# Clustered attention and two feed-forward layers on one core: values and sums in four 32-column strips, one sum for both halves

## The chip, the cores and the metric

The kernel runs on one core of a Trainium2 chip. The metric is the device time of one launch in microseconds (us), here the median of three runs. The engines are TensorE (PE in the profile, PEld for its weight loads), VectorE (DVE), ScalarE (ACT), GpSimd (POOL) and SyncE (SP, which issues the transfers). All of them run their own instruction streams and wait for one another through semaphores.

## The reference

Attention with clusters, then two feed-forward layers, all in float32. Batch 2, 8 heads, 768 positions, 64 values per head, 16 clusters.

```python
q_assign = argmax(einsum('bhsd,hcd->bhsc', q_n, c_n))      # the same for k
mask = q_assign[:, :, :, None] == k_assign[:, :, None, :]
scores = where(mask, scale * (q @ k.T), -1e9)
attn = exp(scores - max(scores))
attn = attn / (attn.sum(-1) + 1e-9)
x = (attn @ v)                                              # to (1536, 512)
h = x @ w_in                                                # 512 -> 2048
g = where(h >= 1, h, where(h <= -1, 0, (h + 1) ** 2 / 4))
x = g @ w_out                                               # 2048 -> 512
xn = x / rms(x) * rms_g
out = (silu(xn @ w_gate) * (xn @ w_val)) @ w_out2           # 512 -> 1536 -> 512
```

## The kernel before

The 16 pairs of batch and head are worked on two at a time: a pair `p` (0 to 7) holds two heads `h`. Its 768 queries are cut into two halves of 384 (`HALF`), its 768 keys into six tiles of 128 (`kt`). A step `i` of a pair is one half and one key tile, so a pair has 12 steps; steps are counted through all pairs as `g` (0 to 95).

In one step `score` (L376) makes, for each head, a 128x384 tile of scores by two matmuls (L382, L383, the second adds the rows of the maxima), and ScalarE takes the exponential into a tile `P` of its own per head (L385, 14 buffers). GpSimd adds the six `P` of a half and head into `acc` (L391, L395). `values` (L397) multiplies `P` by v: each head writes 64 rows of the PSUM tile `pv`, with 64 weight columns (L403); both heads' matmuls run side by side in the array. A float32 matmul is two instructions, two passes over the columns. `values_out` (L414) copies `pv` to SBUF as `pvs`. When a half is through, `sums` (L419) adds `acc` over the 128 partitions by a matmul with a 128x64 tile of ones: each head fills 64 rows of the PSUM tile `sum`, the sum repeated in each row. `finish` (L425) makes the reciprocal and the quotient in six pieces: 0 is logarithm and exponential on ScalarE (L434, L435), 1 and 2 correct it on VectorE in PSUM (L437, L439), 3 multiplies it by the values (L442), 4 and 5 split the product into a rounded part on ScalarE (`xh`, L444) and the rest on VectorE (`xl`, L446), which are what the feed-forward projections read. The last pair takes its sums directly from `P` (L411).

Around this, each step also searches the maxima of a later pair (`maxq` L313: two matmuls L333 into two PSUM banks, each emptied by a VectorE reduction, L335; a bank is written again for the next step only after its reduction), and `prep` (L145) prepares a still later pair: similarities in four strips of 32 columns (L168), a one-hot code on VectorE (L192 to L209), a split of q and k with a subtraction on GpSimd (L160), and copies by transfers on SP's queue (L67).

The order is written out by hand. `attention_steps` (L897) takes two or three steps at a time; three (`by_three`) from step 24 to 83. Of such a group the order on TensorE is: maxima and scores of the first step, scores with the maxima between them of the second, scores and then maxima of the third, and then `values_of` (L886), which puts the sums that are due ahead of the values of the group before. After each step `other_engines` (L862) issues the pieces of `finish` that are due: they are listed as distances `d` from the last step `s` of the half. Piece 0 comes right after the sums in groups of three, and piece 4 at the head of a group. Since each engine's queue is in order, a piece on VectorE stands ahead of the reductions of the step that follows. From step 84 on weights of the feed-forward layers are converted between the steps, and from step 92 some projections (L583) stand between the groups. After step 101 only feed-forward work is left.

Of the kernel before, what the change touches and what calls it, by code (L numbers as in the profile page):

```python
# [9 lines left out]
F32 = mybir.dt.float32  # L10
# [11 lines left out]
DM = H * D  # L22
# [15 lines left out]
def clustered_attention_two_ffn(  # L38
# [43 lines left out]
    ones = cp.tile([128, 64], F32, name="ones")  # L82
# [32 lines left out]
    def p_tile(name, dt=F32):  # L115
        return ap.tile([128, HALF], dt, tag="P", bufs=14, name=name)

# [19 lines left out]
    def one_rows():  # L137

        row = BB[0][96:97, 0, 1]
        nc.scalar.copy(row.rearrange("p (a b) -> p a b", b=64), ones[96:97].unsqueeze(1).to_broadcast([1, S // 64, 64]))  # L140
        copy(BB[0][96:97, 1, 1], row)
        for t in BB[1:]:
            copy(t[96:97, :, 1], row.unsqueeze(1).to_broadcast([1, 2, S]))
# [232 lines left out]
    def score(p, i, h):  # L376
# [7 lines left out]
        P = p_tile(f"P{p}_{i}_{h}")  # L384
        nc.scalar.activation(P, sc, AF.Exp, scale=0.125)  # L385
        st["P", p, i, h] = P
        if p == NP - 1:
            return
        if kt == 1:
            acc = ap.tile([128, HALF], F32, tag="acc", bufs=4, name=f"acc{p}_{i}_{h}")  # L390
            nc.gpsimd.tensor_tensor(acc, st["P", p, i - 1, h], P, op=ALU.add)  # L391
            st["acc", p, half, h] = acc
        elif kt > 1:
            acc = st["acc", p, half, h]
            nc.gpsimd.tensor_tensor(acc, acc, P, op=ALU.add)  # L395

    def values(p, i):  # L397
# [4 lines left out]
        for h in range(2):  # L402
            nc.tensor.matmul(pv[64 * h:64 * h + 64, 0:HALF], st["v", p][:, h, kt], st["P", p, i, h],  # L403
                             start=(kt == 0), stop=(kt == NT - 1))

        if p == NP - 1:
# [3 lines left out]
            for h in range(2):  # L410
                nc.tensor.matmul(st["sm", p, half][64 * h:64 * h + 64], ones, st["P", p, i, h],  # L411
                                 start=(kt == 0), stop=(kt == NT - 1))

    def values_out(p, half):  # L414
        x = ap.tile([128, HALF], F32, tag="fin", bufs=4, name=f"pvs{p}_{half}")
# [3 lines left out]
    def sums(p, half):  # L419
        sm = misc(f"sum{p}_{half}", "sum")[:, 0:HALF]  # L420
        for h in range(2):
            nc.tensor.matmul(sm[64 * h:64 * h + 64], ones, st["acc", p, half, h], start=True, stop=True)  # L422
        st["sm", p, half] = sm

    def finish(p, half, piece):  # L425
        b, hp = divmod(p, 4)
        sm = st["sm", p, half]
        cs = slice(S * b + HALF * half, S * b + HALF * half + HALF)
        xh, xl = XH[:, hp, cs], XL[:, hp, cs]

# [716 lines left out]
```

## Time and profile before

| | |
|---|---|
| median of three runs | 791.8 us (791.02 to 791.87) |
| span of the profiled execution | 789.3 us |
| TensorE busy | 783.0 us (99%) |
| VectorE busy | 569.1 us (72%) |
| ScalarE busy | 353.4 us (45%) |
| GpSimd busy | 167.6 us (21%) |
| mean granted TensorE clock | 1.000 |

The page gives the span from the first to the last instruction; the time of the profiled execution around it isn't given. Busy time is the union of an engine's instructions. The ends of matmuls are modelled, so the distance from start to start tells more of TensorE than busy time does. The attention stage fills the first 235 us or so, the rest is feed-forward work.

### The profile page before, as it was taken

The page shows a single profiled execution, that of the slowest core. Times are in us where ns is not written, and L with a number is a line of the kernel's source. Part 1 is how long each engine was busy: PE and PEld are TensorE (multiplying, and loading weights), DVE is VectorE, ACT ScalarE, POOL GpSimd, SP SyncE. Part 2 cuts the span into 40 slices and gives each one's busy share as a digit, 9 for nine tenths or more (in the row PEclk, how much of TensorE's full clock was granted, in tenths as well). Part 3 has the DMA queues.
Part 4 walks back from the last instruction along what each step waited for, and adds up shares of the span by engine and source line. Part 5 has one row for each costly group of instructions (what it writes and reads, how often), then busy time and mean ns, then how long its engine had stood idle before and what let it go on. Part 6 is the DMA issues. An engine that isn't in the chain of part 4 may idle for free.

```text
span 789.3 us, 10670 instructions
## 1 busy us (share of the span) xinstructions
PE 783.0 (99%) x3786; PEld 605.9 (77%) x3786; DVE 569.1 (72%) x1081; ACT 353.4 (45%) x666; POOL 167.6 (21%) x186
## 2 busy tenths in 40 slices
PE   8999999999999999999999999999999999999998
PEld 4666676676568888888888878888888888888887
DVE  6767787776676878777778788988777888733333
ACT  7676676765566555434444435333333222211110
POOL 5878999997000000000000000000000000000000
PEclk9999999999999999999999999999999999999999
DMA  7756675581333555454443520536555544200003
GB/s 201 175 138 171 161 179 123 138 215 38 107 120 106 173 175 165 158 158 150 143 137 130 161 81 27 159 108 196 175 190 187 159 153 149 73 1 1 1 32 129
DMA packets 32677, 103.40 MB, mean 131 GB/s; under 512 B 5016, under 2 KB 5356, under 8 KB 32624
## 3 DMA queue, kind: packets, MB, share of 16 engines
q1 hardware_dynamic: 32612, 102.72, 44.0%
q8 instruction: 30, 0.49, 0.3%
q14 instruction: 23, 0.19, 0.1%
q10 hardware_dynamic: 12, 0.00, 0.0%
HBM read 81.02 MB, written 3.15 MB: 107 GB/s over the span
## 4 chain that ended last, share of the span: by engine, by line
PE 92%; DVE 4%; ACT 3%; issue 0%; ACTq 0%; DVEq 0%
PE h L583 38%; PE y L631 9%; PE y L632 9%; PE y L633 9%; PE pv L403 8%; PE mp L333 5%; PE sc L382 4%; PE sc L383 4%; PE sum L422 1%; DVE a L603 1%; PE simt L168 1%; ACT a L599 1%; ACT a L598 1%; PE xt L701 1%; PE sum L411 1%; PE oht_ps L219 0%
## 5 line engine op out<-in xcount | busy, mean ns | idle before, releaser
L335 DVE TENSOR_REDUCE M<-mp 128x1 f32<-128x384 f32 x186 | 94.5, 551 | 43.8 <-PE mp L333 43.6
L583 PE MATMUL h<-xh,aa 128*128 128x512 f32 x360 | 116.0, 391 | 0.1
L395 POOL TENSOR_TENSOR acc<-acc,P 128x384 f32<-128x384 f32 x112 | 109.3, 1010 | 4.1 <-ACT P L385 3.5
L583 PE MATMUL h<-xh,bb 128*128 128x512 f32 x312 | 100.9, 389 | 0.1
L385 ACT ACTIVATE P<-sc 128x384 f32<-128x384 f32 x192 | 82.4, 490 | 40.1 <-PE sc L383 32.8
L583 PE MATMUL h<-xh,place 128*128 128x512 f32 x288 | 92.7, 389 | 0.0
L534 ACT ACTIVATE raw<-raw 128x512 f32<-128x512 f32 x62 | 42.1, 679 | 107.7 <-DVE bits L532 105.4
L648 DVE TENSOR_TENSOR Y<-y,Y 128x512 f32<-128x512 f32 (+1 forms) x85 | 57.7, 680 | 31.2 <-PE y L633 31.2
L583 PEld LDWEIGHTS h<-xh,aa 128*128 128x128 f32 x360 | 67.6, 188 | 16.0 <-issue 1.2
L403 PE MATMUL pv<-P,v 128*64 128x384 f32 x384 | 70.6, 492 | 0.0
L583 PE MATMUL h<-xl,aa 128*128 128x512 f32 x180 | 70.1, 389 | 0.0
L583 PEld LDWEIGHTS h<-xh,bb 128*128 128x128 f32 x312 | 58.5, 188 | 12.7 <-DVE bb L546 0.6
L382 PE MATMUL sc<-aa,bb 112*128 112x384 f32 x192 | 66.2, 345 | 0.0
L383 PE MATMUL sc<-aa,bb 97*128 97x384 f32 x192 | 65.0, 338 | 0.0
L603 DVE SCALAR_TENSOR_TENSOR a<-h,a 128x512 f32<-128x512 f32 x48 | 33.1, 690 | 41.9 <-ACT a L599 41.7
L583 PEld LDWEIGHTS h<-xh,place 128*128 128x128 f32 x288 | 54.0, 188 | 11.3
L583 PE MATMUL h<-xl,bb 128*128 128x512 f32 x156 | 60.7, 389 | 0.0
L583 PE MATMUL h<-xl,place 128*128 128x512 f32 x144 | 56.0, 389 | 0.0
L333 PE MATMUL mp<-bb,aa 112*128 112x384 f32 x186 | 52.5, 360 | 0.3
L403 PEld LDWEIGHTS pv<-P,v 128*64 128x64 f32 x384 | 25.4, 136 | 31.5 <-issue 30.3
L532 DVE SCALAR_TENSOR_TENSOR bits<-raw,bits 128x512 uint32<-128x512 uint32 x68 | 46.8, 688 | 1.3
L608 ACT CAST bb<-a 128x512 fp32r<-128x512 f32 x34 | 21.1, 622 | 53.2 <-DVE a L606 33.5
(207 smaller groups left out, 1538.4 us busy)
## 6 DMA issues: line engine op xcount, KB each, us to landing
raw<-w_out SPq DMA_DIRECT2D x28, 512.0 KB
mid<-w_out SPq DMA_DIRECT2D x28, 511.8 KB
raw<-w_in SPq DMA_DIRECT2D x16, 512.0 KB
mid<-w_in SPq DMA_DIRECT2D x16, 511.8 KB
raw<-w_gate SPq DMA_DIRECT2D x12, 512.0 KB
raw<-w_val SPq DMA_DIRECT2D x12, 512.0 KB
mid<-w_gate SPq DMA_DIRECT2D x12, 511.8 KB
mid<-w_val SPq DMA_DIRECT2D x12, 511.8 KB
```

Source lines behind the costliest of these rows:

```text
L333: nc.tensor.matmul(mp, A[0:112, h, 0, 128 * qt:128 * qt + 128], Bk[0:112, h, 0, HALF * n:HALF * n + HALF], start=True, stop=True)
L335: nc.vector.tensor_reduce(st["M2", p][:, j, n:n + 1], mp, axis=AX.X, op=ALU.max)
L382: nc.tensor.matmul(sc, Bk[0:112, h, 0, ks], A[0:112, h, 0, qs], start=True, stop=False)
L383: nc.tensor.matmul(sc, Bk[0:97, h, 1, ks], A[0:97, h, 1, qs], start=False, stop=True)
L385: nc.scalar.activation(P, sc, AF.Exp, scale=0.125)
L395: nc.gpsimd.tensor_tensor(acc, acc, P, op=ALU.add)
L403: nc.tensor.matmul(pv[64 * h:64 * h + 64, 0:HALF], st["v", p][:, h, kt], st["P", p, i, h], start=(kt == 0), stop=(kt == NT - 1))
L583: nc.tensor.matmul(h, w[:, wi, fs], x[:, kc, cs], start=(n == 0), stop=(n == 11))
L631: nc.tensor.matmul(y[:, c], g[:, 0, fs], w[:, 0, c], start=(m == m0), stop=False)
L632: nc.tensor.matmul(y[:, c], g[:, 0, fs], w[:, 1, c], start=False, stop=False)
L633: nc.tensor.matmul(y[:, c], g[:, 1, fs], w[:, 0, c], start=False, stop=(m == ms[-1]))
L648: nc.vector.tensor_tensor(Y[:, c], y[:, c], Y[:, c], op=ALU.add)
```

## The change

Values and sums use four strips of 32 weight columns instead of two of 64. Strips 0 and 2 hold the first and second 32 values of head 0, strips 1 and 3 those of head 1, so that the rows of `pv` run head 0, head 1, head 0, head 1; the rows of `w_in` are put in the same order on the host. The sums of both halves of a pair are made at once: half 0 in rows 0 to 63 (32 for each head), half 1 in rows 64 to 127. Pieces 0 and 1 then run once for a pair. Piece 2 writes the reciprocals twice to SBUF (tiles `R`, one for each half), and a new piece 6 copies the 64 rows that a half has to the 64 that it lacks by a transfer within SBUF on SP's queue. Pieces 3 to 5 work on `pvs` in SBUF instead of on `sum` in PSUM. The two heads' `P` and `acc` share tiles, and GpSimd adds both in one instruction of 768 columns (apart in the first half of pair 0). The last pair keeps its way, in four strips. The distances of the pieces are set anew.

```diff
-    def p_tile(name, dt=F32):
-        return ap.tile([128, HALF], dt, tag="P", bufs=14, name=name)
+    def p_tile(name):
+        return ap.tile([128, 2, HALF], F32, tag="P", bufs=8, name=name)
...
+        apart = p == 0 and half == 0
+        hs = slice(h, h + 1) if apart else slice(0, 2)
+        if h == 0 and kt == 1:
+            st["acc", p, half] = ap.tile([128, 2, HALF], F32, tag="acc", bufs=3, name=f"acc{p}_{half}")
+        if h == 1 or apart:
+            acc = st["acc", p, half]
+            nc.gpsimd.tensor_tensor(acc[:, hs], (st["P", p, i - 1] if kt == 1 else acc)[:, hs], P[:, hs], op=ALU.add)
 
     def values(p, i):
...
-        for h in range(2):
-            nc.tensor.matmul(pv[64 * h:64 * h + 64, 0:HALF], st["v", p][:, h, kt], st["P", p, i, h],
-                             start=(kt == 0), stop=(kt == NT - 1))
+        strips = [(32 * c, c % 2, slice(32 * (c // 2), 32 * (c // 2) + 32)) for c in range(4)]
+        for r, h, d in strips:
+            nc.tensor.matmul(pv[r:r + 32, 0:HALF], st["v", p][:, h, kt, d], st["P", p, i][:, h],
+                             start=(kt == 0), stop=(kt == NT - 1), tile_position=(0, r))
...
-    def sums(p, half):
-        sm = misc(f"sum{p}_{half}", "sum")[:, 0:HALF]
-        for h in range(2):
-            nc.tensor.matmul(sm[64 * h:64 * h + 64], ones, st["acc", p, half, h], start=True, stop=True)
-        st["sm", p, half] = sm
+    def sums(p):
+        sm = misc(f"sum{p}", "sum")[:, 0:HALF]
+        for half in range(2):
+            for h in range(2):
+                r = slice(64 * half + 32 * h, 64 * half + 32 * h + 32)
+                nc.tensor.matmul(sm[r], ones, st["acc", p, half][:, h], start=True, stop=True,
+                                 tile_position=(0, r.start))
+        st["sm", p, 0] = sm
...
         elif piece == 2:
-            nc.vector.scalar_tensor_tensor(sm, sm, 2.0, st["r0", p], op0=ALU.subtract, op1=ALU.mult)
+            for i in range(1 if last else 2):
+                r = sm if last else ap.tile([128, HALF], F32, tag="R", bufs=2, name=f"R{p}_{i}")
+                nc.vector.scalar_tensor_tensor(r, sm, 2.0, st["r0", p], op0=ALU.subtract, op1=ALU.mult)
+                st["R", p, i] = r
         elif piece == 3:
-            nc.vector.tensor_tensor(sm, sm, st["pvs", p, half], op=ALU.mult)
+            if last:
+                nc.vector.tensor_tensor(sm, sm, st["pvs", p, half], op=ALU.mult)
+            else:
+                nc.vector.tensor_tensor(x, x, st["R", p, half], op=ALU.mult)
         elif piece == 4:
-            nc.scalar.activation(xh, sm, AF.Copy, scale=-1.0)
+            nc.scalar.activation(xh, x, AF.Copy, scale=-1.0)
+        elif piece == 6:
+            for i in range(2):
+                t = st["R", p, i]
+                nc.sync.dma_start(t[64 - 64 * i:128 - 64 * i], t[64 * i:64 * i + 64])
         else:
-            nc.vector.scalar_tensor_tensor(xl, sm, -1.0, xh.bitcast(F32), op0=ALU.mult, op1=ALU.subtract)
+            nc.vector.scalar_tensor_tensor(xl, x, -1.0, xh.bitcast(F32), op0=ALU.mult, op1=ALU.subtract)
...
-            for p in range(NP):
-                for half in range(2):
-                    s = 12 * p + 6 * half + 5
-                    ds = (3, 4, 4, 5, 5, 6) if p == NP - 1 else (None, 8, 9, 9, None, 10) if by_three(s) else (7, 8, 9, 10, None, 11)
-                    if ds[piece] == g - s:
-                        finish(p, half, piece)
+            for half in range(2):
+                s = 12 * NP - 7 + 6 * half
+                if (3, 4, 4, 5, 5, 6)[piece] == g - s:
+                    finish(NP - 1, half, piece)
+        for p in range(NP - 1):
+            s = 12 * p + 11
+            late = 3 * (p < NP - 2)
+            for d, half, piece in ((7, 0, 0), (8, 0, 1), (9, 0, 2), (10, 0, 6), (12 + late // 3, 0, 3), (13 + late // 3, 1, 3),
+                                   (14 + late, 0, 5), (16 + late, 1, 5)):
+                if d == g - s and (piece or not by_three(s)):
+                    finish(p, half, piece)
...
-            if 0 <= sp < NP - 1 and si in (5, 11):
-                sums(sp, si // 6)
+            if 0 <= sp < NP - 1 and si == 11:
+                sums(sp)
...
+        for k in range(g, g + n):
+            for half in range(2):
+                for fp_ in range(NP - 1):
+                    if k - 12 * fp_ - 11 == 13 + 3 * half + 3 * (fp_ < NP - 2):
+                        finish(fp_, half, 4)
...
+    def strips(w):
+        return w.reshape(H // 2, 2, 2, D // 2, -1).transpose(0, 2, 1, 3, 4).reshape(DM, -1)
...
-        "w_in": cols(a["moe_w_in"]),
+        "w_in": cols(strips(a["moe_w_in"])),
...
-    nc = _bacc.Bacc("TRN2", target_bir_lowering=False, num_devices=1)
+    nc = _bacc.Bacc("TRN2", target_bir_lowering=False, num_devices=1, dynamic_dma_scratch_size=1024)
```

Left out are the tile of ones (32 columns instead of 64), the same strips in the last pair's sums, the tags of `pvs` and `r0`, and the head of `finish`, which takes `x` as `pvs` of the half and, for the last pair, as `sum`.

## Rows read from the trace of the kernel before

**Rows 1.** The page: the span, and each engine's busy us, share, instructions.

```profile
span 789.3 us, 10670 instructions
PE 783.0 (99%) x3786; PEld 605.9 (77%) x3786; DVE 569.1 (72%) x1081; ACT 353.4 (45%) x666; POOL 167.6 (21%) x186
```

**Rows 2.** Busy time by stretch of the span; columns are in the first line.

```profile
core 0: us, PE busy (x) PEld busy (x) DVE busy (x) ACT busy (x) POOL busy (x), PEclk, DMA share, GB/s
85.00:202.00 117.00, 117.00 (x689) 79.75 (x688) 86.79 (x182) 76.70 (x176) 101.41 (x99) 1.00 0.56 138
```

**Rows 3.** Timeline of TensorE: start, duration (us), engine, line, operation, tiles, shape, count.

```profile
100.25 2.16 PE L403 MATMUL pv<-P,v 128*64 128x384 f32 x12
...
106.04 0.87 PE L422 MATMUL sum<-acc,ones 128*64 128x384 f32 x4
106.74 2.10 PE L403 MATMUL pv<-P,v 128*64 128x384 f32 x12
```

**Rows 4.** Timeline of TensorE, similarities of a later pair in four strips.

```profile
120.70 0.52 PE L168 MATMUL simt<-qraw,CB 128*32 128x384 f32 x2
120.71 0.52 PE L168 MATMUL simt<-kraw,CB 128*32 128x384 f32 x2
121.05 0.49 PE L168 MATMUL simt<-qraw,CB 128*32 128x384 f32 x2
...
121.48 0.44 PE L333 MATMUL mp<-bb,aa 112*128 112x384 f32 x1
```

**Rows 5.** Timeline, TensorE's weight loads for the values of two steps.

```profile
60.94 0.20 PEld L403 LDWEIGHTS pv<-P,v 128*64 128x64 f32 x4 [0.25 <-issue]
...
61.31 0.14 PEld L403 LDWEIGHTS pv<-P,v 128*64 128x64 f32 x2 [0.18 <-issue]
...
61.63 0.14 PEld L403 LDWEIGHTS pv<-P,v 128*64 128x64 f32 x2 [0.18 <-issue]
```

**Rows 6.** Timeline of GpSimd; in brackets idle time before, and what ended it.

```profile
91.33 6.80 POOL L395 TENSOR_TENSOR acc<-acc,P 128x384 f32<-128x384 f32 x7
99.28 1.02 POOL L391 TENSOR_TENSOR acc<-P,P 128x384 f32<-128x384 f32 x1 [1.15 <-ACT P L385]
...
104.95 5.85 POOL L395 TENSOR_TENSOR acc<-acc,P 128x384 f32<-128x384 f32 x6
```

**Rows 7.** Timeline, the first transfer and the instruction that it released.

```profile
0.74 0.39 SPq L108 DMA_DIRECT2D cw<-cent  x1
...
2.43 0.26 ACT L471 ACTIVATE cw<-cw 128x64 f32<-128x64 f32 x1 [0.42 <-DMA cw<-cent]
```

**Rows 8.** Timeline of VectorE in steps 39 to 44.

```profile
105.97 1.02 DVE L335 TENSOR_REDUCE M<-mp 128x1 f32<-128x384 f32 x2 [0.39 <-PE mp L333]
...
109.25 1.02 DVE L335 TENSOR_REDUCE M<-mp 128x1 f32<-128x384 f32 x2
110.19 0.55 DVE L209 TENSOR_TENSOR oh<-sim,m 128x384 bf16<-128x384 f32 x1
110.67 1.02 DVE L335 TENSOR_REDUCE M<-mp 128x1 f32<-128x384 f32 x2
```

**Rows 9.** Timeline of TensorE, maxima matmuls of steps 43 and 44.

```profile
110.29 0.51 PE L333 MATMUL mp<-bb,aa 112*128 112x384 f32 x2
...
111.70 0.52 PE L333 MATMUL mp<-bb,aa 112*128 112x384 f32 x2
```

**Rows 10.** Timeline of GpSimd and VectorE in the first 10 us.

```profile
5.20 0.82 POOL L965 CAST aa<-qhl 64x768 fp32r<-64x768 f32 x1 [2.04 <-ACT qhl L156]
6.08 1.45 POOL L261 CAST aa<-qhl 64x768 fp32r<-64x768 f32 x1
7.61 1.80 POOL L160 TENSOR_TENSOR khl<-kraw,khl 128x768 fp32r<-128x768 f32 x1
...
5.83 1.00 DVE L160 TENSOR_TENSOR qhl<-qraw,qhl 128x768 fp32r<-128x768 f32 x1
```

**Rows 11.** By line, two VectorE products of pair 0: ns least/median/most, first and last start.

```profile
L201 DVE TENSOR_TENSOR e<-eq,rank x1: 627/627/627, 9.0 to 9.0; 128x384 bf16<-128x384 bf16 x1
...
L209 DVE TENSOR_TENSOR oh<-e,m x1: 557/557/557, 10.3 to 10.3; 128x384 bf16<-128x384 bf16 x1
```

More of the change, by code (lines that the diff above doesn't have):

```diff
@@ L81, in clustered_attention_two_ffn @@
     ident_b = cp.tile([128, 128], BF16, name="ident_b")
-    ones = cp.tile([128, 64], F32, name="ones")
+    ones = cp.tile([128, 32], F32, name="ones")
     nc.vector.memset(ones, 1.0)
@@ L139, in one_rows @@
         row = BB[0][96:97, 0, 1]
-        nc.scalar.copy(row.rearrange("p (a b) -> p a b", b=64), ones[96:97].unsqueeze(1).to_broadcast([1, S // 64, 64]))
+        nc.scalar.copy(row.rearrange("p (a b) -> p a b", b=32), ones[96:97].unsqueeze(1).to_broadcast([1, S // 32, 32]))
         copy(BB[0][96:97, 1, 1], row)
@@ L383, in score @@
         nc.tensor.matmul(sc, Bk[0:97, h, 1, ks], A[0:97, h, 1, qs], start=False, stop=True)
[L384 to L387, printed above, removed]
-            return
[L389 to L395, printed above, removed]
+        if h == 0:
+            st["P", p, i] = p_tile(f"P{p}_{i}")
+        P = st["P", p, i]
+        nc.scalar.activation(P[:, h], sc, AF.Exp, scale=0.125)
+        if p == NP - 1 or kt == 0:
+            return
+        apart = p == 0 and half == 0
[5 more added lines that the diff above has]
+            nc.gpsimd.tensor_tensor(acc[:, hs], (st["P", p, i - 1] if kt == 1 else acc)[:, hs], P[:, hs], op=ALU.add)
     def values(p, i):
@@ L409, in values @@
                 st["sm", p, half] = misc(f"sum{p}_{half}", ("misc", "mx1")[half])[:, 0:HALF]
-            for h in range(2):
-                nc.tensor.matmul(st["sm", p, half][64 * h:64 * h + 64], ones, st["P", p, i, h],
-                                 start=(kt == 0), stop=(kt == NT - 1))
+            for r, h, d in strips:
+                nc.tensor.matmul(st["sm", p, half][r:r + 32], ones, st["P", p, i][:, h],
+                                 start=(kt == 0), stop=(kt == NT - 1), tile_position=(0, r))
     def values_out(p, half):
-        x = ap.tile([128, HALF], F32, tag="fin", bufs=4, name=f"pvs{p}_{half}")
+        x = ap.tile([128, HALF], F32, tag="pvs", bufs=4, name=f"pvs{p}_{half}")
         nc.scalar.copy(x, st["pv", p][:, 0:HALF])
         st["pvs", p, half] = x
-    def sums(p, half):
-        sm = misc(f"sum{p}_{half}", "sum")[:, 0:HALF]
-        for h in range(2):
-            nc.tensor.matmul(sm[64 * h:64 * h + 64], ones, st["acc", p, half, h], start=True, stop=True)
-        st["sm", p, half] = sm
+    def sums(p):
[6 more added lines that the diff above has]
+        st["sm", p, 0] = sm
     def finish(p, half, piece):
         b, hp = divmod(p, 4)
-        sm = st["sm", p, half]
+        last = p == NP - 1
+        sm = st["sm", p, half if last else 0]
         cs = slice(S * b + HALF * half, S * b + HALF * half + HALF)
         xh, xl = XH[:, hp, cs], XL[:, hp, cs]
+        x = sm if last else st["pvs", p, half]
         if piece == 0:
-            r0 = st["r0", p] = ap.tile([128, HALF], F32, tag="fin", bufs=4, name=f"r0{p}_{half}")
+            r0 = st["r0", p] = ap.tile([128, HALF], F32, tag="r0", name=f"r0{p}_{half}")
             nc.scalar.activation(r0, sm, AF.Ln, bias=eps9)
@@ L901, in attention_steps @@
             max_rows(*row, 1)
-        fp_, fi = divmod(g - (10 if n == 3 else 11), 12)
-        if 0 <= fp_ < NP - 1 and fi in (5, 11):
-            finish(fp_, fi // 6, 4)
+        for k in range(g, g + n):
[3 more added lines that the diff above has]
+                        finish(fp_, half, 4)
         for k in range(g, g + n):
```

2 lines of the change are left out of this document (1 added, 1 removed).

## The prediction, made before the changed kernel had been run

> **What bounds the kernel now.** I read the page first: TensorE is busy 783.0 of 789.3 us, VectorE 569.1, GpSimd 167.6 [rows 1]. GpSimd's small share hides a stage: by stretches, between 85 and 202 us TensorE has no idle time, while GpSimd works 101.41 of 117 us, VectorE 86.79 and ScalarE 76.70, with the granted clock at 1.00, the 2.4 GHz level [rows 2]. So in the attention stage TensorE sets the pace, GpSimd runs close behind, and VectorE has about 30 us of air, unevenly spread. The change touches only this stage; the projections behind it start earlier by whatever it saves. Where TensorE starts late on a VectorE result, that shows as an idle gap before a maxima matmul; in the stretch that I read instruction by instruction (97 to 122 us, one pair's period of 12 steps) there is none. Hence TensorE work taken out should count in full, and any new delay of VectorE beyond its cover counts in full too.
>
> **Part 1, sums (the gain).** A group of steps with a sum: its matmuls begin at 106.04 and the values at 106.74, and those last 2.10; without a sum the values last 2.16 [rows 3]. So a sum costs 0.70 - 0.06 = 0.64 us. Today each half of the seven pairs before the last has its sum, 14 in all; the change keeps seven. That takes out 7 x 0.64 = **4.5 us**, all on TensorE's path.
>
> **Part 2, four strips.** Half the columns per matmul, twice the matmuls. If strips run side by side, a pass over 384 columns costs the same. The similarity matmuls show four strips of 32: the first pass starts at 120.70, the second at 121.05, and all of one pass start together [rows 4]. For today's two strips of 64 the weight loads show the rhythm: 0.37 us from the first pass to the second, then 0.32 [rows 5]. I read 0.05 of the 0.37 as the first weight load, which nothing covers; for 32 columns it is then 0.35 - 0.32 = 0.03. Per entry that saves 0.03, and the last of four strips starts about 0.01 later than the last of two; 38 groups x 0.017 = 0.6 us gained. The similarity matmuls that follow values would no longer change strip width; leaving a width costs some 0.1 beyond a pass (121.48 less 121.05 is 0.43 [rows 4]), six times at most, so 0 to 0.6; I take 0.5. Together **-1.1 us**. The other end: a steady third pass of four strips is not in the trace. If every pass took 0.35 instead of 0.32, 216 passes (192 for values, 24 for the last pair's sums) would lose 0.025 x 216 = 5.4 us. I take the first end, since the longer interval is explained by its weight load.
>
> **Part 3, GpSimd's adds.** Two adds of 384 become one of 768 (five pairs at the start stay apart). Six adds in a row last 5.85, about 0.97 each [rows 6]; a subtraction of 768 lasts 1.80 [rows 10]. One for two saves about 0.1 us, some 6 us in all on GpSimd, which is not the bound. The sum now waits for an add that starts only with the second head and ends up to 1.80 - 0.97 = 0.8 later. Cover: the last add of a half ends at 91.33 + 6.80 = 98.13 [rows 6], its sum starts at 106.04 [rows 3], 7.9 us. Cost nothing; the larger ring of P tiles only loosens ScalarE.
>
> **Part 4, finishing.** ScalarE loses seven logarithm and exponential pairs, VectorE seven first corrections: idle time, no gain. The 14 transfers sit in SP's queue behind the second corrections, and place copies and weight loads wait behind them. A transfer is issued three steps (about 6 us) ahead of its reader, two for pair 6. The nearest landing: a first transfer issued at 0.74 releases ScalarE at 2.43, 1.7 us later [rows 7]. Hidden; were that cover gone, the product would stand on VectorE with the next reductions behind it, and TensorE behind those: up to about 1.7 us a pair. In the tail pair 6 finishes at step 97, while the projections of token block 0, which does not read it, are still on TensorE: nothing.
>
> What is not hidden is where VectorE's pieces land. Steps run in threes. Steps 39 to 41 have one piece in place of another, and the idle 0.39 before 105.97 takes it [rows 8]. But step 42 (as 30, 54 and 66) now has the low part and the one-hot ahead of the second pair of maxima: the reductions at 110.67 move by one piece (0.48 by 110.19 to 110.67), end at 112.17, and the second matmul of the pair at 111.70 is due at 111.87 [rows 8, 9]. That is 0.3 late in each of the four periods that have a one-hot, **+1.2 us**.
>
> **Part 5, VectorE against GpSimd.** The product (values times reciprocal) and the low part used to have one input in PSUM; now both are in SBUF. The trace has such instructions only in its first 10 us, and there they touch. GpSimd's copy of 64x768 takes 0.82 alone and 1.45 when VectorE's two-input subtraction (5.83 to 6.83) starts first [rows 10]: GpSimd stood until VectorE was done. The other way round, a two-input product of VectorE, begun while GpSimd's 1.8 us subtraction ran, took 627 ns against 557 for its neighbour [rows 10, 11]: 0.07 us lost.
>
> Nine such pieces lie where VectorE has little cover while GpSimd is busy: in four periods one before the one-hot chain (cover 0.2: the reductions at 109.25 end at 110.27, due 110.46 [rows 8, 9]) and one at step 42 (no cover left); in the fifth period one. The two earlier pieces of a period fall into GpSimd's pause (98.13 to 99.28 [rows 6]) or start just ahead of its next add. By the 0.07 of the nearest row: 9 x 0.07 = **+0.6 us**. The upper end is a wait for a whole add of 768, 1.8 by the subtraction's row: 9 x 1.8 less the cover of 0.2 at five of them, 15.2 us. I take the low end because it is the only row in that direction, and keep the other for the range.
>
> The Trainium skill, page "SBUF — State Buffer", section "Who interferes with whom", says that a VectorE instruction with two SBUF inputs contends with a GpSimd instruction that reads SBUF, and that whichever issues first blocks the other completely. By that rule VectorE would wait for the rest of an add, and the case called "port" below would hold; the 1.45 agrees with the rule in one direction, the 627 shows little of it in the other.
>
> **Sum.** -4.5 - 1.1 + 1.2 + 0.6 = -3.8 us. The profiled execution has a span of 789.3; its time around the span is not shown, so I carry over the 2.5 us between the span and the median of 791.8. Span after 785.5, time **788.0 us**.
>
> **Rivals.** *Port, bad phase (slower).* VectorE stands behind a whole add. GpSimd's adds follow each other without a pause, so the place in its cycle at which a piece arrives repeats from pair to pair. A piece at step 40 that just misses an add waits about 1.5, less 0.2 of cover, and one at step 42, half an add later, about 0.9: 4 x 2.2 + 0.7 = 9.5 instead of 0.6, so -3.8 + 8.9 = +5.1: 796.9. For it: the 1.45, GpSimd's 87% in this stretch, adds twice as long. Against: the 627. It decides from 0.5 us lost per piece (4.4 of net gain without the port, over nine).
> *Port, mean phase (no change).* Pieces arrive at random in a 1.8 us cycle of which the port is held for about 1.5 (an estimate: the product that began 0.4 before the subtraction's end lost only 0.07, so the end of it is free): mean wait 1.5 x 1.5 / (2 x 1.8) = 0.63, behind the cover 0.47; 4 x 1.1 + 0.5 = 4.9: 792.3.
> *Strips slower.* The 5.4 of part 2 instead of its 0.6: -3.8 + 6.0 = +2.2: 794.0, slower. Against it: strips of one pass start together today.
> That the change doesn't do what it says would need sums to wait for GpSimd; the 7.9 us speak against it, under 2 in 100.
>
> **How the numbers follow.** About 0.2% (1.6 us) is what a measurement here can tell from no change. Forecast 0.42, its own range 785.5 to 789.8; port in mean phase 0.20; port in bad phase 0.30; strips 0.08. Faster 0.42, same 0.20, slower 0.38. The range of 8 in 10 reaches from 785.4 (parts 1 and 2 with no late piece, 786.2, less 0.8, the spread of the three runs) to 797.7 (port in bad phase and the same 0.8).
>
> **What would show it.** Right: sums in seven groups instead of 14; passes of values 0.32 apart; no idle before maxima matmuls; products and low parts near 0.55 us. Port: those two lines at 1 us and more or with VectorE idle before them, and TensorE's maxima released by VectorE late at steps 30, 42, 54 and 66. Strips: passes 0.35 apart. I would be wrong altogether if a transfer came later than its reader, or if TensorE's gain vanished in a wait that no row here shows.

## Result and the profile after

The changed kernel takes 802.8 us (median; 799.3 to 803.0) against 791.8 us before: ratio 1.0127, 95% interval 1.0107 to 1.0147. It is slower by 11 us, where 788.0 was forecast and the range ended at 797.7. The profiled execution is the shortest of them, 799.34 us with a span of 797.5, 8.2 over before's span [rows 1]; the traces are compared on these two.

The page: span, then each engine's busy time. Below them, from TensorE's list of waits (us in total, times, longest), the two kinds that the kernel before does not have.

```profile
span 797.5 us, 11359 instructions
PE 784.4 (98%) x4218; PEld 602.0 (75%) x4218; DVE 574.9 (72%) x1074; ACT 347.5 (44%) x652; POOL 164.0 (21%) x121
...
PE mp L333 <- DVE M L335: 5.1, 5, 1.2
PE mp L333 <- DMA bb<-oht: 1.0, 2, 0.8
```

TensorE's maxima matmuls now wait for VectorE's maxima and for one-hot copies. Busy time by stretch answers [rows 2]: of the 117 us that TensorE filled before, 6.5 are idle.

```profile
core 0: us, PE busy (x) PEld busy (x) DVE busy (x) ACT busy (x) POOL busy (x), PEclk, DMA share, GB/s
85.00:202.00 117.00, 110.50 (x854) 72.87 (x855) 87.52 (x166) 67.44 (x155) 98.70 (x53) 0.99 0.59 146
...
85.00:88.10 3.10, 1.85 (x8) 1.28 (x8) 3.10 (x5) 1.80 (x5) 3.10 (x2) 1.00 0.97 203
88.20:91.60 3.40, 3.40 (x18) 1.26 (x22) 2.81 (x7) 0.00 (x0) 3.32 (x3) 0.50 0.86 225
```

The last row is a second loss. Behind a stretch in which TensorE was busy 1.85 of 3.10 us, its granted clock was 0.50, the 1.2 GHz level, from 88.2 to 91.6. At half speed 3.4 us of work is 1.7 us lost, by estimate. Three later waits of nearly the same length (1.22, 1.23 and 1.13 us, at 115.09, 140.63 and 167.94) were followed by no fall.

By line (busy us, mean ns of one): low part and product, after and then before; the sums, after and then before.

```profile
L463 DVE SCALAR_TENSOR_TENSOR xl<-pvs,xh 128x384 fp32r<-128x384 f32 x13 | 15.5, 1194 | 1.4 <-ACT xh L457 1.4
L455 DVE TENSOR_TENSOR pvs<-pvs,R 128x384 f32<-128x384 f32 x14 | 10.4, 740 | 0.0
...
L446 DVE SCALAR_TENSOR_TENSOR xl<-sum,xh 128x384 fp32r<-128x384 f32 x15 | 8.2, 548 | 3.5 <-ACT xh L444 3.5
L442 DVE TENSOR_TENSOR sum<-sum,pvs 128x384 f32<-128x384 f32 x16 | 9.0, 563 | 0.4
...
L426 PE MATMUL sum<-acc,ones 128*32 128x384 f32 x56 | 6.0, 498 | 0.0
L422 PE MATMUL sum<-acc,ones 128*64 128x384 f32 x56 | 12.1, 512 | 0.0
```

The sums came down as meant. The low part went from 548 to 1194 ns. One of its instructions, by the timelines of VectorE, GpSimd and TensorE (start, duration):

```profile
85.24 1.89 DVE L463 SCALAR_TENSOR_TENSOR xl<-pvs,xh 128x384 fp32r<-128x384 f32 x1
87.06 0.54 DVE L209 TENSOR_TENSOR oh<-sim,m 128x384 bf16<-128x384 f32 x1
87.53 1.00 DVE L335 TENSOR_REDUCE M<-mp 128x1 f32<-128x384 f32 x2
...
82.98 3.73 POOL L396 TENSOR_TENSOR acc<-acc,P 128x768 f32<-128x768 f32 x2
86.67 2.13 POOL L160 TENSOR_TENSOR qhl<-qraw,qhl 128x768 fp32r<-128x768 f32 x1
...
88.12 1.15 PE L333 MATMUL mp<-bb,aa 112*128 112x384 f32 x2 [1.24 <-DVE M L335]
```

The second of GpSimd's two adds ends at 86.71; the low part, begun some 0.35 us into it, ends 0.42 later. Its neighbours last 0.55: it stood 1.34 us. All 16 products and low parts of this trace that began while a GpSimd instruction ran ended 0.41 or 0.42 us after the end of that instruction; those that began beside none, or just ahead of one, took 0.54 to 0.56. The one-hot and the reductions behind the low part are late by the 1.34, and TensorE is idle for 1.24. The low part is that of step 30, the matmul that of step 32. It comes again at 42, 54 and 66, where the same matmul starts 1.38, 1.39 and 1.29 us later than in the rhythm of its neighbours (1.40 here).

The other loss, by SyncE's queue (SPq) and TensorE, in a later pair:

```profile
148.76 1.23 SPq L461 DMA_DIRECT2D R<-R  x2
150.03 1.23 SPq L67 DMA_DIRECT2D aa<-qhl  x2
151.71 0.34 SPq L134 DMA_DIRECT2D v<-vP  x1
152.16 1.17 SPq L67 DMA_DIRECT2D aa<-oht  x2
153.37 1.22 SPq L67 DMA_DIRECT2D bb<-oht  x2
...
156.84 0.58 PE L333 MATMUL mp<-bb,aa 112*128 112x384 f32 x2 [0.79 <-DMA bb<-oht]
```

Two transfer issues hold SyncE's queue for 1.23 us, and the one-hot copies come out of the same queue behind them. They are not alone there: the two maxima copies ahead of them took 2.62 us to issue (from 146.04), where those of the period before took 1.46. And of the 1.0 us in the list of waits, 0.21 fell at 53.97, before the first of these transfers (69.86); so 0.79 at most is theirs.

The account, from the start of each step's first score matmul, after less before: -0.9 us at step 24, -1.0 at 30, +2.8 at 33, +2.0 at 36, +3.8 at 45, +3.0 at 48, +4.7 at 57, +3.9 at 60, +7.5 at 69, +6.8 at 72, +7.6 at 84, +8.2 at the end. Each dropped sum gives 0.7 to 0.8 (33 to 36, 45 to 48, 57 to 60, 69 to 72); every group of steps with a late low part takes 1.8 to 3.8 more than before. The other executions have a mean clock of 0.991 to 0.996 where this one has 0.998. An estimate from that: 6 to 14 us at the half level instead of 3.4, so 1.5 to 5.5 us more, where 3.5 was measured. One by one it does not fit (802.86 us at 0.996, 803.01 at 0.991), so what else makes them longer stays open.

### The profile page after: what moved, and what is told of

Its sections match the earlier page's. It is cut to its first block, busy times and chain, and to the rows that moved or that the text cites. A ratio compares the mean times of both kernels' runs of the same rounds, so it can differ in the third digit from the quotient of the medians.

```text
span 797.5 us, 11359 instructions
## 1 busy us (share of the span) xinstructions
PE 784.4 (98%) x4218; PEld 602.0 (75%) x4218; DVE 574.9 (72%) x1074; ACT 347.5 (44%) x652; POOL 164.0 (21%) x121
## 4 chain that ended last, share of the span: by engine, by line
PE 84%; DVE 10%; ACT 3%; issue 1%; DMA 1%; SPq 0%; ACTq 0%; DVEq 0%
PE h L600 37%; PE y L648 9%; PE y L650 9%; PE y L649 9%; PE pv L405 6%; PE mp L333 4%; PE sc L382 3%; PE sc L383 3%; DVE M L335 2%; DVE xl L463 1%; DVE a L620 1%; PE simt L168 1%; DMA bb<-oht 1%; PE xt L718 1%; ACT P L387 1%
## 5 line engine op out<-in xcount | busy, mean ns | idle before, releaser
L396 POOL TENSOR_TENSOR acc<-acc,P 128x768 f32<-128x768 f32 (+1 forms) x60 | 104.9, 1749 | 16.9 <-ACT P L387 13.4
L405 PE MATMUL pv<-P,v 128*32 128x384 f32 x768 | 71.9, 497 | 0.0
L333 PE MATMUL mp<-bb,aa 112*128 112x384 f32 x186 | 55.7, 371 | 6.7 <-DVE M L335 5.1
L333 PEld LDWEIGHTS mp<-bb,aa 112*128 112x128 f32 x186 | 32.4, 190 | 26.8 <-DVE M L335 13.7
L405 PEld LDWEIGHTS pv<-P,v 128*32 128x32 f32 x768 | 22.0, 111 | 33.1 <-issue 31.1
```

The costliest lines, as they stand in the source:

```text
L333: nc.tensor.matmul(mp, A[0:112, h, 0, 128 * qt:128 * qt + 128], Bk[0:112, h, 0, HALF * n:HALF * n + HALF], start=True, stop=True)
L396: nc.gpsimd.tensor_tensor(acc[:, hs], (st["P", p, i - 1] if kt == 1 else acc)[:, hs], P[:, hs], op=ALU.add)
L405: nc.tensor.matmul(pv[r:r + 32, 0:HALF], st["v", p][:, h, kt, d], st["P", p, i][:, h], start=(kt == 0), stop=(kt == NT - 1), tile_position ...
```

## The experiments

Where the time went in each kernel, from its trace: steps 24 to 84 (first score matmul to first score matmul), TensorE's idle time in them, and the time that it spent there at the half clock level. The ratio is to the kernel before, run on the same chip beside it. The medians of e2 and e3 stand for wide ranges, 797.5 to 807.8 and 797.9 to 809.2, and their traces are of long executions.

| kernel | median us | ratio, 95% interval | steps 24-84 | idle | at half level |
|---|---|---|---|---|---|
| before | 791.8 | | 121.2 | 0.2 | 0 |
| the change | 802.8 | 1.0127 [1.0107, 1.0147] | 129.7 | 6.7 | 3.4 |
| e1_no_adds | 792.0 | 0.9998 [0.9978, 1.0017] | 123.3 | 2.5 | 3.4 |
| e2_adds_apart | 805.4 | 1.0134 [1.0076, 1.0192] | 138.4 | 10.9 | 13.7 |
| e3_before_low_sbuf | 807.1 | 1.0166 [1.0103, 1.0229] | 133.8 | 8.1 | 10.2 |
| e4_low_from_psum | 800.1 | 1.0101 [1.0076, 1.0127] | 130.5 | 6.2 | 10.2 |
| e5_act_queue | 802.8 | 1.0143 [1.0129, 1.0158] | 132.8 | 8.1 | 6.8 |
| e8_no_adds_act | 794.8 | 1.0031 [1.0020, 1.0043] | 125.5 | 4.9 | 0 |
| e7_r_in_psum | 800.2 | 1.0097 [1.0082, 1.0113] | 127.4 | 6.3 | 0 |
| e9_r_in_psum_sp | 796.9 | 1.0052 [1.0040, 1.0064] | 124.9 | 5.1 | 0 |
| e11_no_copies | 798.4 | 1.0069 [1.0053, 1.0085] | 127.7 | 4.7 | 3.4 |
| e10_strips_only | 791.3 | 0.9993 [0.9980, 1.0005] | 123.1 | 1.8 | 0 |
| e12_engine_copies | 793.7 | 1.0022 [1.0013, 1.0031] | 120.7 | 1.3 | 0 |
| e13_copies_moved | 793.1 | 1.0013 [1.0003, 1.0024] | 121.2 | 1.6 | 0 |

**First group.** Three theories: *port* (VectorE instructions with two SBUF inputs wait for GpSimd), *crowding* (the pieces' new steps make VectorE late whatever GpSimd does), *transfers* (SyncE's queue is late).

e1 leaves out GpSimd's adds from the third key tile on:

```diff
-        if h == 1 or apart:
+        if (h == 1 or apart) and kt == 1:
```

> The changed kernel with GpSimd's adds of the third to sixth P tile of each half left out (only the first two tiles are added, so the sums lack four of six tiles; GpSimd keeps its subtractions). Theory port (a VectorE piece with two SBUF inputs waits for the GpSimd instruction in flight): low parts fall from a mean of 1.19 us to 0.55 to 0.7, products to 0.55, the maxima matmuls at the third step of groups 30, 42, 54 and 66 are no longer 1.3 us late, time 786 to 789. Rival crowding (too many VectorE pieces ahead of the reductions, no matter what GpSimd does): low parts stay near 1.2 or their wait moves into the reductions, time 800 to 803. Rival transfers (SP's queue is held up by the new transfers): time 800 to 803, the late one-hot copies stay.

792.0 us: 10.9 us of the loss went with the adds, and the list of waits has no maxima matmul behind VectorE any more. By line:

```profile
L463 DVE SCALAR_TENSOR_TENSOR xl<-pvs,xh 128x384 fp32r<-128x384 f32 x14 | 7.7, 550 | 1.4 <-ACT xh L457 1.4
L455 DVE TENSOR_TENSOR pvs<-pvs,R 128x384 f32<-128x384 f32 x14 | 7.7, 550 | 0.1
```

The same instructions at the same steps last 550 ns without adds beside them: as the main cause, crowding falls. A rest of it stands. The groups from steps 30, 42, 54 and 66 still take 6.25 or 6.26 us against 5.83 to 5.85 before, 1.7 us in sum, because the second of the two maxima matmuls of their third step starts later behind the first. No idle time is listed for it; the pair lasts longer. The pair of step 56 in e1, and then in before:

```profile
137.98 0.90 PE L333 MATMUL mp<-bb,aa 112*128 112x384 f32 x2
...
136.27 0.52 PE L333 MATMUL mp<-bb,aa 112*128 112x384 f32 x2
```

And 786 to 789 was expected. One gap of 1.8 us before a maxima matmul at 103.31 (it ends about when the one-hot copies come in) and 3.4 us at the half level behind it are left: the port is not all.

e2 keeps the changed kernel, with every add split into two of 384:

```diff
-        apart = p == 0 and half == 0
+        apart = True
```

> The changed kernel with one add of 384 for each head instead of one of 768 for both, as before the change. Theory port: the longest wait is for one add, so it halves from 1.35 to 0.7 us; low parts at 0.8 to 0.9 on average, TensorE late by at most 0.7 at each place, time 793 to 797. Rival crowding: no change, 800 to 803. Rival transfers: no change.

805.4, no better. Timelines of VectorE, GpSimd and TensorE, and a stretch:

```profile
105.28 7.10 DVE L463 SCALAR_TENSOR_TENSOR xl<-pvs,xh 128x384 fp32r<-128x384 f32 x1
...
104.39 5.82 POOL L396 TENSOR_TENSOR acc<-acc,P 128x384 f32<-128x384 f32 x6
110.18 1.79 POOL L160 TENSOR_TENSOR qhl<-qraw,qhl 128x768 fp32r<-128x768 f32 x1
...
112.91 1.15 PE L333 MATMUL mp<-bb,aa 112*128 112x384 f32 x2 [4.31 <-DVE M L335]
...
113.40:120.10 6.70, 6.59 (x21) 5.30 (x25) 5.91 (x13) 2.95 (x6) 2.79 (x3) 0.50 0.66 199
```

My expectation took the wait for the rest of one add. The low part stood through the rest of the six adds and the whole subtraction behind them, 7.1 us. TensorE stood 4.31, and then ran at the half level from 113.4 to 120.1. So the port theory holds, but the wait is not always bounded by one GpSimd instruction: two low parts stood that long (7.10 and 7.07), while eleven other pieces of this trace stood only until the add in flight was done (they took 0.59 to 1.23).

e3 takes the kernel before and changes nothing but where the product goes: to SBUF, where the rounded part (its line is not shown) and the low part read it.

```diff
-            nc.vector.tensor_tensor(sm, sm, st["pvs", p, half], op=ALU.mult)
+            x = st["pvs", p, half]
+            nc.vector.tensor_tensor(x, sm, x, op=ALU.mult)
...
-            nc.vector.scalar_tensor_tensor(xl, sm, -1.0, xh.bitcast(F32), ...)
+            nc.vector.scalar_tensor_tensor(xl, st["pvs", p, half], -1.0, xh.bitcast(F32), ...)
```

> The kernel before with one edit: the product of values and reciprocal goes to SBUF (over the values) instead of PSUM, so that the low part has two SBUF inputs; nothing else moves. Theory port: low parts rise from 0.55 to 0.7 to 1.1 where GpSimd adds, and since they stand ahead of the second step's reductions, TensorE is late by up to 0.7 at some of 10 places: time 793 to 798. Rival crowding: as many pieces in the same places, so no change, 791 to 792.5.

807.1, far over the 793 to 798 expected: this alone costs 15 us by the median (the interval reaches from 8 to 18), as much as the whole change or more. VectorE, GpSimd and TensorE again:

```profile
107.98 8.80 DVE L447 SCALAR_TENSOR_TENSOR xl<-pvs,xh 128x384 fp32r<-128x384 f32 x1
...
107.04 1.85 POOL L160 TENSOR_TENSOR khl<-kraw,khl 128x768 fp32r<-128x768 f32 x1
108.84 5.77 POOL L395 TENSOR_TENSOR acc<-acc,P 128x384 f32<-128x384 f32 x6
114.55 1.82 POOL L160 TENSOR_TENSOR qhl<-qraw,qhl 128x768 fp32r<-128x768 f32 x1
...
117.31 1.15 PE L333 MATMUL mp<-bb,aa 112*128 112x384 f32 x2 [7.66 <-DVE M L335]
```

The low part stood through the rest of one subtraction, six adds and a second subtraction. No transfer, no strip and no new step is in this kernel, so the second SBUF input is enough.

e4 writes the changed kernel's product into the bank of the sums (PSUM), from which the low part reads; the product still has two SBUF inputs. Since a bank holds one half at a time, the steps move too: the first product one step sooner, the low parts four and three steps sooner.

```diff
-                nc.vector.tensor_tensor(x, x, st["R", p, half], op=ALU.mult)
+                nc.vector.tensor_tensor(sm, st["pvs", p, half], st["R", p, half], op=ALU.mult)
```

> The changed kernel with the product written back to the sum's PSUM bank, so that the low part has one SBUF input again; as the bank holds one half at a time, the halves follow each other (product at distance 12 and 14, rounded part 13 and 16, low part 13 and 16). Theory port: low parts at 0.55, the late maxima gone, the granted clock at 1.00 through the attention stage, time 786 to 789. Rival crowding: one piece less at step 42, so some 1.2 us of 11 come back, 800 to 802. Rival transfers: the product reads one step sooner than now, so it would stand with a transfer as what released it, time above 795.

800.1. By line, and from VectorE's waits:

```profile
L463 DVE SCALAR_TENSOR_TENSOR xl<-sum,xh 128x384 fp32r<-128x384 f32 x14 | 7.7, 547 | 0.6 <-ACT xh L457 0.6
L455 DVE TENSOR_TENSOR sum<-pvs,R 128x384 f32<-128x384 f32 x14 | 12.2, 871 | 14.3 <-DMA R<-R 14.3
...
DVE sum L455 <- DMA R<-R: 14.3, 4, 5.8
```

The low part is cured (547 ns), and the product stands on the transfer, four times, up to 5.8 us: the third theory's loss, which the late steps of the change avoid. The wait is mostly one in the queue: the reciprocals read by the product at 99.62 were written by 90.89, and their first transfer was issued at 97.43. The product also still lasts 871 ns beside the adds. The port's 786 to 789 did not come; the two losses are not told apart in this run.

**Second group.** Port and transfers are now both suspects. e5 and e8 issue the transfers on ScalarE's queue; e8 also leaves out the adds as e1 does.

```diff
-                nc.sync.dma_start(t[64 - 64 * i:128 - 64 * i], ...)
+                nc.scalar.dma_start(t[64 - 64 * i:128 - 64 * i], ...)
```

> The changed kernel with one edit: the 14 transfers of the reciprocals are issued on ScalarE's queue instead of SyncE's. Theory now: three losses add up in the changed kernel, the waits of VectorE's two-SBUF-input pieces for GpSimd (TensorE idle 6.7 us before maxima in its trace), one-hot copies that stand behind the transfers in SyncE's queue (1.0 us), and a half granted clock after long waits. By it this edit takes away only the second: 798 to 802 us, the gaps of TensorE that end with a one-hot copy gone, those that end with a VectorE maximum still there. Rival, SyncE's queue is the main cause (VectorE's waits for GpSimd would be hidden otherwise): under 791 us.

> The changed kernel without GpSimd's adds from the third key tile on (the sums are then of two tiles only), and with the transfers on ScalarE's queue: both suspects removed together. Without the adds alone the time was 792.0 us, with TensorE gaps of 1.5 and 0.3 us that ended with a one-hot copy. Theory (port and SyncE's queue together are the whole loss): 785.5 to 788 us, no gap of TensorE over 0.5 us before a maximum in the stage, granted clock 1.00 throughout it. Rival 1, the gaps after one-hot copies have nothing to do with the transfers in the queue: 790 to 792.5 as without the adds alone. Rival 2, the transfers now hold up ScalarE's exponentials: 790 or more with TensorE gaps before values.

e5: 802.8; TensorE's waits, ScalarE's queue and TensorE's timeline:

```profile
PE mp L333 <- DVE M L335: 4.9, 4, 1.3
PE sc L382 <- ACT P L387: 2.9, 5, 0.7
...
94.88 1.20 ACTq L461 DMA_DIRECT2D R<-R  x2
...
96.73 0.44 PE L382 MATMUL sc<-aa,bb 112*128 112x384 f32 x1 [0.55 <-ACT P L387]
```

As expected, the waits for the port stay, and from the first transfer on no maxima matmul waits for a one-hot copy. But the two issues hold ScalarE for 1.20 us, and once a pair a score waits for the exponential behind them. The trace has the half level twice, from 89.0 to 92.4 and from 143.6 to 147.0, and a span of 801.1, like the longer executions of the change.

e8: 794.8, more than e1 (whose two gaps before one-hot copies were 1.75 and 0.55 us in this stage, not the 1.5 and 0.3 of the expectation). Its rival 2 holds (2.2 us of scores waiting for ScalarE), and one gap is longer:

```profile
104.74 0.59 PE L333 MATMUL mp<-bb,aa 112*128 112x384 f32 x2 [2.34 <-DMA bb<-oht]
```

The one-hot copies were issued by 100.59, as early as in before (100.55). Their last rows came late: in the trace's DMA packets one 16 KB packet of the instruction queue runs from 101.84 to 103.27, and the next one-hot row starts at 103.27. In before such a packet ran at 103.76, after the copies. So the issue was not late; that the packet held the rows back fits the times and was not tried. After it the clock stayed at 1.00.

e7 computes everything and avoids the port: ScalarE copies the transferred reciprocals into the bank of the sums, product and low part read that bank.

```diff
+        elif piece == 7:
+            nc.scalar.copy(sm, st["R", p, half])
...
-                nc.vector.tensor_tensor(x, x, st["R", p, half], op=ALU.mult)
+                nc.vector.tensor_tensor(sm, sm, st["pvs", p, half], op=ALU.mult)
```

> The changed kernel with the port avoided instead of the adds taken out: ScalarE copies each half's reciprocals from SBUF into the bank of the sums (PSUM), VectorE's product and low part read that bank, so that each has one SBUF input; transfers on ScalarE's queue; steps 13, 14, 14 and 15, 16, 16 after the pair's last group for product, high and low part of the two halves. All of the result is computed. Theory (port and SyncE's queue are the whole loss): products and low parts at 0.54 to 0.58 us beside GpSimd's adds, no long gap of TensorE, 785.5 to 788.5 us, faster than both kernels. Rival 1, GpSimd's adds disturb VectorE in another way than by the second SBUF input: 796 or more. Rival 2, ScalarE's 14 copies (0.45 us each) and its waits for the transfers hold up its exponentials: 789 to 794, with VectorE's pieces short and TensorE waiting for ScalarE.

800.2: the pieces last 555 and 560 ns beside GpSimd's full work and no maxima matmul waits for VectorE, yet the theory's number did not come. The time lies where rival 1 put it (796 or more), but rival 1's disturbance of VectorE is not there. Scores wait for ScalarE (2.5 us) and maxima copies (1.4), maxima matmuls for one-hot copies (2.8): rival 2's mechanism and late copies. From step 94 to the end this kernel and e9 also take 572.8 us against 569.9 before, so not all of the loss is in the stage.

**Third group.** e9 is e7 with the transfers on SyncE's queue, one step sooner; e11 is e9 without ScalarE's copies, so that the product has two SBUF inputs again; e10 is the kernel before with strips alone.

```diff
 e9:  -  nc.scalar.dma_start, at step 10      +  nc.sync.dma_start, at step 9
 e11: -  nc.scalar.copy(sm, st["R", p, half])
      -  tensor_tensor(sm, sm, st["pvs", p, half])   +  tensor_tensor(sm, st["pvs", p, half], st["R", p, half])
 e10: -  for h in range(2): nc.tensor.matmul(pv[64 * h:64 * h + 64, 0:HALF], st["v", p][:, h, kt], ...)
      +  for r, h, d in strips: nc.tensor.matmul(pv[r:r + 32, 0:HALF], st["v", p][:, h, kt, d], ..., tile_position=(0, r))
```

> The run e7_r_in_psum with the transfers back on SyncE's queue and issued one step sooner (step 9 in place of 10, ahead of the maxima rows and the next one-hot copies in that queue). In e7 VectorE's pieces lasted 0.56 us and the clock stayed at 1.00 in the stage, yet it took 800 us: TensorE's scores waited 0.6 to 0.7 us once a pair for ScalarE behind its two transfer issues (1.2 us), and 4.2 us for one-hot and maxima copies. Theory (what is left of the loss is the place of the transfers): steps 24 to 84 in at most 119.5 us (before 121.2, the change 129.7, e7 127.4), no wait of a score for ScalarE, 787.5 to 790 us. Rival 1, the stage has no room for 14 transfers of 96 KB on any queue, since its copies collide in the DMA engines: a gap of 1 us or more that ends with a one-hot or a maxima copy, 791 to 797. Rival 2, ScalarE waiting for the transfer itself holds the scores: 791 to 797 with TensorE waiting for ScalarE.

> The run e9_r_in_psum_sp without ScalarE's copies: the product reads values and reciprocals from SBUF (two SBUF inputs) and writes the bank of the sums; everything else at the same steps. All of the result is computed. Port theory: the six to seven pairs have 14 products that can meet GpSimd's adds, some of them last 1 to 2 us in place of 0.55, and the time is 1 to 6 us over that of e9, with TensorE waiting for VectorE's maxima. Rival, only the low parts in their late steps cost time and the products stand where VectorE has cover: within 0.8 us of e9. If ScalarE's copies are what costs in e9: this one faster than e9 by over 0.8 us.

> The kernel before with one part of the change alone: values and sums in four strips of 32 columns (with the matching order of the rows of w_in). Sums, adds, finishing and their steps stay as before, so each half has its own sum and nothing is transferred. By part 2 of the prediction (0.03 us per entry and 0.5 for the strip widths): 790.5 to 791.5, against 792.1 before. By the changed kernel's trace, whose end from step 94 on took 0.7 us longer than before: 791 to 792.5. Rival, strips cost 0.025 us a pass: 795 to 798.

e9: 796.9, its rival 1: no score waits for ScalarE any more, and 3.1 us of waits for one-hot and 1.4 for maxima copies stay. e11: 798.4, 1.5 more by the medians (the ranges, 796.2 to 797.0 and 796.5 to 800.0, overlap); the product by line, e9 and then e11:

```profile
L455 DVE TENSOR_TENSOR sum<-sum,pvs 128x384 f32<-128x384 f32 x14 | 7.8, 561 | 1.5 <-ACT sum L459 1.5
...
L455 DVE TENSOR_TENSOR sum<-pvs,R 128x384 f32<-128x384 f32 x13 | 11.9, 913 | 0.0
```

The port's price shows on the product alone. e10: 791.3 against 792.3, an interval that includes no change; from step 39 to step 84 its trace gains 0.6 us on before, and a gap of 1.6 before a one-hot copy at step 39 hides that. This kernel has no transfer of reciprocals, so a one-hot copy can come late without one: in before those of step 39 already land about when the matmul that reads them starts (102.7).

**Fourth and fifth group.** e12 does without transfers and without second SBUF inputs: one tile of reciprocals, of which ScalarE copies each half's 64 partitions twice into the bank of the sums, once across to the other 64. e13 moves the first two copies of a pair a step sooner and finishes pair 6 in SBUF.

```diff
-                t = st["R", p, i]
-                nc.sync.dma_start(t[64 - 64 * i:128 - 64 * i], t[64 * i:64 * i + 64])
+                nc.scalar.copy(sm[64 * i:64 * i + 64], st["R", p][64 * half:64 * half + 64])
```

> The change without any transfer and without two SBUF inputs: VectorE makes one tile of reciprocals for both halves (one correction fewer per pair), ScalarE copies each half's 64 partitions twice from it into the bank of the sums (PSUM), once to the same partitions and once to the other 64, so that product and low part read PSUM and one SBUF tile. Steps 12 (copies), 13, 14, 14 and 15 (copies), 15, 16, 16; the last finishing pair three steps sooner. All of the result is computed. Theory (port, and transfers that crowd SyncE's queue and the DMA engines, are the whole loss): VectorE's pieces at 0.54 to 0.57 us, steps 24 to 84 in 118 to 120.5 us (before 121.2, the change 129.7), time 786 to 790 us, faster than before. Rival 1, the one-hot and maxima copies have no cover at any faster pace, with or without transfers: a gap of 1 us or more ended by such a copy, 790.5 to 793. Rival 2, four copies of ScalarE a pair (about 0.45 us each) hold the scores: 790.5 to 796 with TensorE waiting for ScalarE.

> The run e12_engine_copies with ScalarE's copies moved where its trace showed TensorE waiting for them: the first two of a pair one step sooner (11 for 12; a similarity matmul waited 0.9 us for the one-hot copy behind them at pair 0), and pair 6 finished as in the changed kernel (values times reciprocals in SBUF, since GpSimd adds nothing there any more) with one copy of 64 partitions per half by ScalarE in place of the transfers, at step 10 (in e12 a projection waited 2.1 us behind its copies). All of the result is computed. Theory: the stage as in e12 or better (steps 24 to 84 in 119.5 to 120.7 us), the 2.1 us down to 0.4 and the 0.9 gone: 790.5 to 792.0 us, about 2 us less than e12. Rival, the waits only move (the one-hot chain and the projections' activations take ScalarE at any step): 792.5 to 794.

e12: 793.7. Its stretch (against 110.50 busy in the change), the two pieces by line, and TensorE's longest waits:

```profile
85.00:202.00 117.00, 116.31 (x938) 77.16 (x934) 83.80 (x176) 82.41 (x187) 97.02 (x54) 1.00 0.56 140
...
L461 DVE SCALAR_TENSOR_TENSOR xl<-sum,xh 128x384 fp32r<-128x384 f32 x15 | 8.2, 554 | 3.5 <-ACT xh L456 3.5
L454 DVE TENSOR_TENSOR sum<-sum,pvs 128x384 f32<-128x384 f32 x14 | 7.9, 561 | 4.3 <-ACT sum L459 4.2
...
PE h L598 <- DVE a L618: 2.1, 1, 2.1
PE simt L168 <- ACT oht L235: 1.6, 4, 1.1
```

Steps 24 to 84 take 120.7 us, 9.0 less than in the change and the first that are shorter than before's. That much of the theory stands: without second SBUF inputs and transfers the stage's loss is gone. Not all of the 9.0 is theirs: e12's steps also take away the 1.7 of e1's groups (they last here as in before), and VectorE makes one correction less a pair, which is not told apart. The whole is still 0.2% slower than before: ScalarE's copies hold a projection for 2.1 us and similarity matmuls for 1.6. e13: 793.1; the 2.1 became 0.6, but one-hot copies came late by 1.9 in sum, without any transfer of reciprocals: its rival, the waits moved. No version was clearly faster than the kernel before.

## Why the prediction was wrong

**Part 1 was right.** Sums fell from 12.1 to 6.0 us of busy time, and each dropped one gives 0.69 to 0.80 where 0.64 was worked out.

**Part 2 was right in the trace.** Passes of four strips start 0.32 us apart, and e10 gains 0.6 us over 45 steps; in the time the 1.1 us is too small to show. Its rival (0.35 a pass) is refuted: e10 would have lost 5.4 (6.5 by the rival's own 0.35 less 0.32).

**Part 3 was right on the sums.** No sum waits for an add. That the row of adds makes VectorE wait was left to part 5.

**Part 5 is the step that failed**, the price of 0.07 us a piece from 627 less 557 ns [rows 11]. Over the trace the low part lost 0.65 us a piece (1194 less 548) and the product 0.18 (740 less 563). The row had met only the last 0.4 us of a GpSimd instruction [rows 10], and I took it for the rule because it was the nearest; the piece at 85.24 began some 0.35 us into an add and stood 1.34. And its neighbour of 557 ns is another instruction and no measure for it. In the changed kernel the same product happens to start when GpSimd's subtraction is done:

```profile
9.69 0.36 DVE L201 TENSOR_TENSOR e<-eq,rank 128x384 bf16<-128x384 bf16 x1
...
6.95 2.40 POOL L160 TENSOR_TENSOR khl<-kraw,khl 128x768 fp32r<-128x768 f32 x1
```

Alone it takes 0.36 us, so in the kernel before it lost 0.27 of the 0.41 that it met. It ended 0.22 us after GpSimd's instruction (9.63 and 9.41), 0.14 less than its own 0.36; the pieces ended 0.41 or 0.42 after theirs, 0.13 to 0.14 less than their 0.55. So the row that was held against the first rival shows the same full wait. The Trainium skill, page "SBUF — State Buffer", section "Who interferes with whom", says that the engine which issues first blocks the other completely: the 1.34 agrees, and the 7.10 of e2 goes beyond the one instruction of its wording.

**The first rival had the mechanism, and its number only in part.** The places were right (steps 30, 42, 54, 66), with 1.3 us at step 42 where it had 0.9. But the piece of step 40, which it priced at 1.3 in each of four periods, cost TensorE nothing (steps 39 to 42 take 0.01 us less than before, and none of the three like groups more than 0.01 more). What it left out came instead: the half clock level (1.7 us in the profiled execution), the late one-hot copies (0.8 at most) and 0.7 at the end. That its 796.9 is as near as 2.4 to the profiled execution is luck; the median is 5.9 over it.

**Part 4 was right on step 42 and failed on the transfers.** The +1.2 us showed: 1.7 in e1, at the four places, without adds. "Hidden" was said of the transfer's reader, and in the change that held (0.0 us of idle time before the product). But the landing of 1.7 us [rows 7] was taken in the idle start of the kernel, and the three steps ahead were counted from the place in the program; in e4 a transfer left the queue 6.5 us after its data was written and its product stood 4.0 us, in another pair 5.8. The copies that wait behind the transfers in SyncE's queue were named and priced at nothing: they cost up to 0.8 us of TensorE's waits in the profiled execution, and e5, without these transfers in that queue, has none of it. How much of the late copies is the transfers' stays open, since e7, e8, e10 and e13 have such waits with none of these transfers in that queue. From e9 to e12, where engine copies replace transfers, the time falls by 3.2 us (2.4 by the ratios), with other steps and one correction less. "In the tail nothing" was off by 0.7: from step 94 to the end 570.6 us against 569.9, and 569.9 again in e10; which piece of the new finishing it is was not tried.

What stays open: why two low parts of e2 and two of e3 stood through a row of GpSimd's instructions, where the other late pieces got in behind the one in flight.

## What to carry to other kernels

Before moving an operand from PSUM to SBUF, count the SBUF inputs of the VectorE instruction that reads it: with two, beside a GpSimd that adds without pause, it stands at least until the add in flight is done and at times through the whole row, and everything in order behind it pays. Where TensorE has no idle time, look for the chains that are just in time (here the one-hot copies): any gain makes them the next bound, and a gap can cost again in the clock. To move data to other partitions, an engine's copy into PSUM went with a shorter time here (e12 against e9) than a transfer whose queue others need, but it too stands in some engine's order.

## What the runs showed of the hardware

- A VectorE instruction with two SBUF inputs that begins while a GpSimd instruction runs waits for it: 16 pieces of the change ended 0.41 or 0.42 us after that instruction, where they take 0.55 alone. With one input in PSUM they last 0.55 to 0.56 beside the same adds.
- Such an instruction can also wait far longer: 7.10 and 8.80 us, through six back-to-back GpSimd adds and one or two subtractions.
- The granted clock fell to 0.50 for 3.4 us behind a stretch with TensorE busy 1.85 of 3.10 us, and for 6.8 us behind the 4.31 us wait of e2; e8's gap of 2.34 us was followed by no fall. The length of one gap alone did not tell.
- Two transfer issues hold the queue that issues them for 1.2 us, on SyncE (1.23) and on ScalarE (1.20) alike.
- A 16 KB packet of the instruction queue (101.84 to 103.27 in e8) ran just before the last rows of a one-hot copy, for which TensorE waited 2.34 us; that it held them back was not tried.
